# Moving weight conversion from the middle of a chunked recurrence into its last steps

## Chip, cores and metric

One core of a Trainium2 chip runs the whole kernel. The metric is the device time in microseconds; the kernel before has a median of 979.26 us over three runs (976.2 to 980.47).

## What is computed

Three layers follow one another. The first is a recurrence over 768 positions with a 40x40 state for each of 4 batches x 8 heads; the second a feed-forward layer with a three-tap convolution and a gate; the third an FFT mixing, a normalisation and a second feed-forward layer.

```python
def _attn_ref(r, k, v, w, a, b):                       # B, H, S, D = 4, 8, 768, 40
    for t in range(S):
        y[:, :, t] = np.einsum('bhd,bhde->bhe', rt, state)
        Sa = np.einsum('bhde,bhe->bhd', state, at)
        state_decay = state * wt[:, :, None, :] - np.einsum('bhd,bhe->bhde', Sa, bt)
        state = state_decay + np.einsum('bhd,bhe->bhde', vt, kt)

def _moe_ref(x, w_in, conv_w, w_out):                  # x: 4 x 768 x 320, w_in: 320 x 1024
    h = np.maximum(x @ w_in, 0.0)
    ...
    for k in range(K):
        conv_out += conv_w[k][None, None, :] * hp[:, k:k + S, :]
    gate = 1.0 / (1.0 + np.exp(-conv_out))
    return (h * gate @ w_out).astype(np.float32)
```

The weights `w_in`, `w_out`, `conv_w`, `w_ch1` and `w_ch2` arrive as 64-bit floats. They are turned into 32-bit floats on the chip, and all but `w_out` and `conv_w` are split into a high and a low part.

## The kernel before, in words

**The recurrence** is cut into 12 chunks of 64 positions. `Attn.run` (its loop is at L663) makes 52 steps n = 0 to 51; step n works on batch n % 4 of chunk n // 4, and on later stages of the three items before it. `step` (L530) writes out the order of the stages: `stage_u`, `stage_h` and `stage_y` interleaved on TensorE (PE), then `stage_s` (state update: `sm` on VectorE, L452 and L456, then `st` on GpSimd, L457 and L458), `stage_g` (`gt` on VectorE, L470), `stage_sb`, `stage_ut` and `stage_o` (`xo` on VectorE, L509, stored by L513). One `gt` and one `xo` stand in each step. The inputs of a chunk's half (`vbd` L203, `z` L183, `zt` L185, `rbd` L187, `r` L191) are loaded by the SyncE queue (SP) every second step, in line with everything else that SP issues.

Beside the steps a triangular inverse for each pair of chunks runs on VectorE (`tmp` and `A`, L333 and L336; its transposes L313, L343, L346). It is spread evenly over the steps until step 40, by when the last pair needs it. After that no step has any of it.

**The conversion** is a second stream of work that `run` takes as `side`. `Moe.prep` (L731) goes through 63 pieces; 30 of them (`NLEFT` leaves 33) lie in the recurrence: 12 of `w_in` (128x256), 16 of `w_out` (128x160) and 2 of `w_ch1` (128x256). `conv_w` (L756) follows. A piece is loaded as `raw` (L765, SP), and then takes these instructions:

```python
raw = tp.tile([128, PC, 2], I32, name="raw", tag="raw", bufs=2)[:p, :w]     # L764, load L765 on SP
nc.scalar.activation(m, hi.bitcast(F32), AF.Abs)                            # L775 ScalarE, pm<-raw
nc.scalar.activation(y, lo.bitcast(U32), AF.Copy, scale=2.0 ** -29)         # L776 ScalarE, py<-raw
nc.vector.tensor_scalar(m, m, W_LEAST, W_MOST, op0=ALU.max, op1=ALU.min)    # L778 VectorE
nc.vector.tensor_scalar(m, m, 3, 0x3fffffff, ...)                           # L780 VectorE
nc.gpsimd.tensor_tensor(m, m, y, op=ALU.add)                                # L782 GpSimd, pm<-pm,py
nc.vector.scalar_tensor_tensor(m, hi, -0x40000000, m, ...)                  # L785 VectorE, pm<-raw,pm
```

A `w_out` piece is then stored by L745. A piece that is split goes on with `wh` (L749, ScalarE, stored by L750) and `wl` (L752, VectorE, stored by L753). `raw` and `pm` have two buffers, `py`, `wh` and `wl` one. The next piece's `raw` is issued when a piece starts.

`prep` is a generator with a `yield` after each group of instructions, 8 to 9 for a piece. `step` is one too, with some 8 to 10 yields a step. At each yield of a step `run` adds `SIDE` to a counter (L681), and for each whole unit in it takes one group from `side`, so `SIDE = 0.75` means three groups for four yields. A group is tied behind the last instruction marked on ScalarE and VectorE (`issue_after`). What is left of `side` when the steps are over is taken at once. A scheduler then makes each engine's order out of this program order and those ties; all engines run their list in order.

**The second layer** begins with `moe1_start` (L821): `load_k320` (L798 to L802) brings the converted `w_in` back from DRAM in six transfers of 2.62 MB together, and L819 brings `w_out` (eight transfers, 1.31 MB). These tiles lie on the same side of the on-chip memory as the tiles of the conversion. `moe1` then loads `xf` (L836 to L838), makes `xh` and `xl` of it (ScalarE L839 to L841, GpSimd L842 to L844), and its first multiplication `hp<-xh,w_in_h` (L701) needs all six `w_in` tiles. `cw`, the convolution's weights, is needed by L876. The 33 pieces left are converted beside this layer.

Of the kernel before, what the change touches and what calls it, by code (L numbers as in the profile page):

```python
# [61 lines left out]
SM = 1  # L62
MG = 1
RI = 0.8
SIDE = 0.75
N1ST = 4
NA = 8
HL = 3
LG = 16
# [5 lines left out]
def turns(left, right):  # L75


    sides = []
    for stages in (left, right):
        ops = []  # L80
        for todo, end in stages:
            ops += [(op, None) for op in todo[:-1]] + [(todo[-1], end)]
        sides.append(ops)
    n = max(len(ops) for ops in sides)
    for k in range(n):
        for ops in sides:
            for op, end in ops[k * len(ops) // n:(k + 1) * len(ops) // n]:
                op()
                if end is not None:
                    end()  # L90
                    yield
# [7 lines left out]
class Attn:  # L99
# [494 lines left out]
    def run(self, side):  # L594
        nc, tc = self.nc, self.tc
        self.start()
        wm = self.pst("warm")
        for _ in range(WARM):
            nc.tensor.matmul(wm[:, 0:396], self.ends[:, 0:128], self.ends, start=True, stop=True)
        self.load_pre(0, 0)  # L600
        nc.sync.dma_start(self.mdiag, self.i["mdiag"])
        self.load_pre(0, 1)
        nc.sync.dma_start(self.mltq, self.i["mlt"])
        nc.sync.dma_start(self.ident, self.i["ident"])
        self.load_pre(1, 0)
        self.grp_start(0)
        self.decay(0, 0)
        for hb in range(2):
            if hb:
                self.decay(0, 1)  # L610
            for bl in range(2):
                self.gram(0, 2 * hb + bl)
        for hb in range(2):
            self.load_v(0, hb)
        self.pads()
        for hb in range(2):
            self.load_z(0, hb)
            self.load_r(0, hb)
        inv = self.inverse(0)
        for n in range(ST0):  # L620
            next(inv)
        for hb in range(2):
            for bl in range(2):
                self.gram_x(0, 2 * hb + bl)
        with tc.issue_after(self.late.ins):
            for hb in range(2):
                self.squares(0, hb)
                if hb == 0:
                    self.load_pre(1, 1)
        self.grp_start(1)  # L630

        def half(hb):
            if hb < ST2:
                self.decay(1, hb)
            else:
                with tc.issue_after(self.first.ins):
                    self.decay(1, hb)
            self.squares(1, hb)
            for bl in range(2):
                self.gram(1, 2 * hb + bl)  # L640
                self.gram_x(1, 2 * hb + bl)
        half(0)
        for b in range(B):
            for _ in turns([self.stage_h(0, b)], []):
                pass
        if ST1:
            half(1)
        next(inv)
        next(inv)
        tr = self.last  # L650
        for _ in inv:
            pass
        if not ST1:
            half(1)
        live, g = [], 1
        for hb in range(2):
            self.load_v(1, hb)
        for k in range(8 - LD, 8 - LG, 2):
            h = divmod((k + LD) // 2, 2)
            self.load_pre(*h)  # L660
            with tc.issue_after(tr.ins):
                self.decay(*h)
            self.squares(*h)  # L663
        sd, na = 0.0, 8 - LG
        for n in range(B * NCH + 4):
            while live and n == live[0]["end"]:
                for _ in live.pop(0)["inv"]:
                    pass
            while g <= NCH // 2 and na + LG >= 8 * g and len(live) < 2:
                end = 8 * g - 8 if g > 1 else 4  # L670
                live.append(dict(inv=self.inverse(g), end=end, last=0, acc=0.0,
                                 rate=RI * (35 if g == 1 else 70) / 7 / max(1, end - n - MG)))
                next(live[-1]["inv"])
                g += 1
            pre = []
            for _ in range(1 + (n < NA)):
                if na <= n:
                    pre.append(self.ahead(na))
                    na += 1
            for _ in self.step(n, itertools.chain(*pre), live):  # L680
                sd += SIDE if n >= N1ST else 0.0  # L681
                while sd > 0:
                    with ExitStack() as st:
                        for m in [self.mark, self.markd][:1 + SM]:
                            if m is not None:
                                st.enter_context(self.tc.issue_after(m.ins))
                        next(side, None)
                    sd -= 1.0
                for k, v in enumerate(live):
                    v["acc"] += v["rate"]  # L690
                    while v["acc"] > 0 and not (v["last"] == "t" and k or v["last"] in ("merge", "join", "done")):
                        v["last"] = next(v["inv"], None)
                        v["acc"] -= 1.0
        for _ in side:
            pass
# [714 lines left out]
```

## Time and profile before

| what | value |
|---|---|
| median of three runs | 979.26 us |
| profiled execution | 977.45 us, span 975.5 us |
| PE busy | 818.7 us (84% of the span) |
| VectorE (DVE) busy | 668.3 us (69%) |
| ScalarE (ACT) busy | 519.7 us (53%) |
| GpSimd (POOL) busy | 433.2 us (44%) |
| first `up` of the recurrence | 72.1 us |
| first `hp` of the second layer | 478.0 us |
| mean granted clock of PE | 0.925 of full speed |

Busy shares of the whole span mix three layers with different limits, so the table serves to find the stages; each stage is read by itself. L12 is line 12 of the kernel; a `pm<-pm` is an instruction that writes the tile `pm` from the tile `pm`. SPq is SyncE, which issues the transfers. In brackets behind a row of a timeline stands how long the engine had been idle before it and what ended that.

### The profile page before, as it was taken

The page shows a single profiled execution, that of the slowest core. Times are in us where ns is not written, and L with a number is a line of the kernel's source. Part 1 is how long each engine was busy: PE and PEld are TensorE (multiplying, and loading weights), DVE is VectorE, ACT ScalarE, POOL GpSimd, SP SyncE. Part 2 cuts the span into 40 slices and gives each one's busy share as a digit, 9 for nine tenths or more (in the row PEclk, how much of TensorE's full clock was granted, in tenths as well). Part 3 has the DMA queues.
Part 4 walks back from the last instruction along what each step waited for, and adds up shares of the span by engine and source line. Part 5 has one row for each costly group of instructions (what it writes and reads, how often), then busy time and mean ns, then how long its engine had stood idle before and what let it go on. Part 6 is the DMA issues. An engine that isn't in the chain of part 4 may idle for free. (4 is left out here: it accounts for less than half of the span.)

```text
span 975.5 us, 21804 instructions
## 1 busy us (share of the span) xinstructions
PE 818.7 (84%) x8178; PEld 745.1 (76%) x8178; DVE 668.3 (69%) x1320; ACT 519.7 (53%) x1448; POOL 433.2 (44%) x507
## 2 busy tenths in 40 slices
PE   5457765776886787877899899899999999999997
PEld 3446655676776787776877677777889999999997
DVE  6994897998997898942378688788773544424321
ACT  4747685577676785543566665656553321312211
POOL 5465355465565553532368557665662130101000
PEclk8758797898898999988999999999999999999999
DMA  9623262566564654539444643213004000000001
GB/s 231 187 57 108 80 172 72 167 172 164 162 175 109 172 138 114 159 101 262 121 123 111 208 122 92 79 29 94 14 26 151 22 1 21 21 21 22 21 14 32
DMA packets 102990, 101.16 MB, mean 104 GB/s; under 512 B 47272, under 2 KB 89115, under 8 KB 102875
## 3 DMA queue, kind: packets, MB, share of 16 engines
q1 hardware_dynamic: 100907, 94.73, 34.7%
q0 software_dynamic: 1968, 4.93, 1.7%
q8 instruction: 67, 1.10, 0.5%
q14 instruction: 48, 0.39, 0.1%
HBM read 74.81 MB, written 20.76 MB: 98 GB/s over the span
## 5 line engine op out<-in xcount | busy, mean ns | idle before, releaser
L1132 DVE SCALAR_TENSOR_TENSOR gl<-hp,gh 128x384 fp32r<-128x384 f32 x80 | 44.4, 556 | 111.3 <-ACT gh L1131 111.2
L895 PE MATMUL acc<-w_out_f,z 128*128 128x320 f32 x384 | 116.6, 441 | 3.6 <-POOL z L882 2.1
L1131 ACT ACTIVATE gh<-hp 128x384 fp32r<-128x384 f32 x80 | 39.3, 492 | 149.7 <-PE hp L701 149.6
L878 DVE SCALAR_TENSOR_TENSOR c<-h,cw,c 128x384 f32<-128x384 f32 x128 | 101.6, 798 | 17.3 <-ACT c L876 15.4
L895 PEld LDWEIGHTS acc<-w_out_f,z 128*128 128x128 f32 x384 | 72.1, 193 | 28.2 <-POOL z L882 3.9
L701 PE MATMUL hp<-xh,w_in_h 128*128 128x386 f32 x192 | 76.4, 398 | 12.1 <-ACT h L869 11.9
L701 PE MATMUL hp<-uh,w_ch_h 128*128 128x384 f32 x240 | 82.3, 343 | 0.0
L701 PE MATMUL hp<-ul,w_ch_h 128*128 128x384 f32 x240 | 81.0, 337 | 0.0
L388 PE MATMUL yp<-x,gt 128*64 128x40 f32 x768 | 64.9, 244 | 18.8 <-DVE gt L470 18.4
L1155 POOL DMA_INDIRECT out<-o,rows x12 | 11.8, 982 | 150.8 <-DVE o L1150 131.9
L388 PEld LDWEIGHTS yp<-x,gt 128*64 128x64 f32 x768 | 60.0, 148 | 21.4 <-DVE gt L470 21.4
L219 PE MATMUL gram<-abd,kb 120*128 120x192 f32 (+1 forms) x288 | 59.5, 353 | 17.8 <-DMA a<-in_a 11.2
L1145 PE MATMUL acc<-w_ch_h,gh 128*128 128x320 f32 x240 | 73.2, 312 | 0.0
L1145 PE MATMUL acc<-w_ch_l,gh 128*128 128x320 f32 x240 | 73.0, 309 | 0.0
L333 DVE TENSOR_TENSOR tmp<-A 128x30 f32<-128x30 f32 (+9 forms) x150 | 70.1, 467 | 3.1
L219 PEld LDWEIGHTS gram<-abd,kb 120*128 120x128 f32 x288 | 55.1, 224 | 19.4 <-issue 11.6
L336 DVE TENSOR_TENSOR A<-A,tmp 128x30 f32<-128x30 f32 (+9 forms) x150 | 67.3, 449 | 2.9
L701 PE MATMUL hp<-xl,w_in_h 128*128 128x386 f32 x192 | 67.4, 351 | 0.0
L388 PE MATMUL gp<-rbd,zt 120*128 120x192 f32 (+1 forms) x288 | 59.0, 347 | 7.1 <-ACT zt L437 4.0
L782 POOL TENSOR_TENSOR pm<-pm,py 128x160 int32<-128x160 int32 (+2 forms) x64 | 44.4, 693 | 41.2 <-DVE pm L780 22.3
L879 ACT ACTIVATE c<-c 128x384 f32<-128x384 f32 x64 | 33.4, 521 | 53.9 <-DVE c L878 53.5
L1145 PE MATMUL acc<-w_ch_h,gl 128*128 128x320 f32 x240 | 61.4, 309 | 0.0
(225 smaller groups left out, 2565.0 us busy)
## 6 DMA issues: line engine op xcount, KB each, us to landing
kb<-in_kb SPq DMA_DIRECT2D x24, 360.0 KB
vbd<-in_vbd SPq DMA_DIRECT2D x24, 320.0 KB
xd<-xo SPq DMA_DIRECT2D x56, 90.0 KB
w<-in_w SPq DMA_DIRECT2D x24, 185.6 KB
a<-in_a SPq DMA_DIRECT2D x24, 180.0 KB
z<-in_zv SPq DMA_DIRECT2D x24, 180.0 KB
zt<-in_vt SPq DMA_DIRECT2D x24, 180.0 KB
rbd<-in_r SPq DMA_DIRECT2D x72, 60.0 KB
```

The source lines that it names most:

```text
L219: nc.tensor.matmul(gp[:, 192 * gi:192 * gi + 64 * nh], d["kb"][:, bl * NG + gi].rearrange("p a b -> p (a b)"), abd[:, 0:nh, bl * NG + gi], ...
L333: nc.vector.tensor_tensor(tmp, A[:, s + 1:32, s:s + 1].to_broadcast([128, n, s]), A[:, s:s + 1, 0:s].to_broadcast([128, n, s]), op=ALU.mult)
L336: nc.vector.tensor_tensor(A[:, s + 1:32, 0:s], A[:, s + 1:32, 0:s], tmp, op=ALU.add)
L388: self.lastpe = op(*args, **kw)
L701: nc.tensor.matmul(out, l, r, start=(j == 0), stop=(j == len(ops) - 1))
L782: nc.gpsimd.tensor_tensor(m, m, y, op=ALU.add)
L878: nc.vector.scalar_tensor_tensor(c, h[:, j:HS + j], cw[:, f, j:j + 1], c, op0=ALU.mult, op1=ALU.add)
L879: nc.scalar.activation(c, c, AF.Sigmoid)
L895: nc.tensor.matmul(self.acc[t][:, 0:DM], z[:, ts], w[:, f], start=(f == 0), stop=(f == NF1 - 1))
L1131: self.mark = nc.scalar.activation(gh, hp[:, 0:HS], AF.Relu)
L1132: nc.vector.scalar_tensor_tensor(gl, hp[:, 0:HS], 0.0, gh.bitcast(F32), op0=ALU.max, op1=ALU.subtract)
L1145: nc.tensor.matmul(self.acc[t][:, 0:DM], l[:, ts], r, start=(f == 0 and j == 0), stop=(f == NF2 - 1 and j == 2))
```

## The change

Two constants are changed and two are new. Up to step 7 no group of the conversion is taken (before: up to step 3); from step 8 to 37 the counter rises by 0.37 a yield, from step 38 on by 2.2.

```diff
-SIDE = 0.75
-N1ST = 4
+SIDE = 0.37
+SIDE2 = 2.2
+N1ST = 8
+N2ST = 38
...
             for _ in self.step(n, itertools.chain(*pre), live):
-                sd += SIDE if n >= N1ST else 0.0
+                sd += (SIDE if n < N2ST else SIDE2) if n >= N1ST else 0.0
                 while sd > 0:
```

No instruction is added or left out; every engine has the same ones in another order. Lines of the changed kernel that lie behind the constants are two higher (L470 becomes L472).

VectorE, around the 29th `gt` of the recurrence, where an inverse ends (L343, L346; `A` and `t` are the inverse's tiles). Before:

```order
L452 TENSOR_TENSOR sm_112<-sp,mdiag 120x240
L456 TENSOR_TENSOR sm_112<-sp,mdiag 80x80
L778 TENSOR_SCALAR pm<-pm 128x160
L780 TENSOR_SCALAR pm<-pm 128x160
L470 TENSOR_TENSOR gt<-gp,mlt 128x512
L343 STREAM_TRANSPOSE t_4951<-A 128x32x32
L346 STREAM_TRANSPOSE tt_132<-A 128x32x32 x2
L509 TENSOR_TENSOR xo<-yt,wx 120x192
L785 SCALAR_TENSOR_TENSOR pm<-raw,pm 128x160
L452 TENSOR_TENSOR sm_112<-sp,mdiag 120x240
```

The same place now:

```order
L454 TENSOR_TENSOR sm_112<-sp,mdiag 120x240
L458 TENSOR_TENSOR sm_112<-sp,mdiag 80x80
L472 TENSOR_TENSOR gt<-gp,mlt 128x512
L345 STREAM_TRANSPOSE t_4777<-A 128x32x32
L348 STREAM_TRANSPOSE tt_132<-A 128x32x32 x2
L511 TENSOR_TENSOR xo<-yt,wx 120x192
L787 SCALAR_TENSOR_TENSOR pm<-raw,pm 128x256
L454 TENSOR_TENSOR sm_112<-sp,mdiag 120x240
```

Two instructions of the conversion have left the row ahead of `gt`, and the piece in hand is one of `w_in` (256 wide), where before it was one of `w_out`. Counted over the lists, 96 of the conversion's VectorE instructions stand before the 36th `gt` in the kernel before (12 pieces of `w_in` and 16 of `w_out`), and 44 in the changed one (11 of `w_in`).

VectorE, in one of the last steps, from an `xo` on. Before:

```order
L509 TENSOR_TENSOR xo<-yt,wx 120x192
L452 TENSOR_TENSOR sm_112<-sp,mdiag 120x240
L456 TENSOR_TENSOR sm_112<-sp,mdiag 80x80
L470 TENSOR_TENSOR gt<-gp,mlt 128x512
L509 TENSOR_TENSOR xo<-yt,wx 120x192
```

Now:

```order
L511 TENSOR_TENSOR xo<-yt,wx 120x192
L787 SCALAR_TENSOR_TENSOR pm<-raw,pm 128x160
L780 TENSOR_SCALAR pm<-pm 128x160
L782 TENSOR_SCALAR pm<-pm 128x160
L787 SCALAR_TENSOR_TENSOR pm<-raw,pm 128x160
L454 TENSOR_TENSOR sm_112<-sp,mdiag 120x240
L458 TENSOR_TENSOR sm_112<-sp,mdiag 80x80
L472 TENSOR_TENSOR gt<-gp,mlt 128x512
```

Four to five VectorE instructions of the conversion stand in each of these steps now, one and a half pieces, where none stood. From the 39th `gt` to the 48th and last the changed list has 46 of them.

SP, at the end of the recurrence, where the weights of the second layer are loaded (`w_in_h_6705` and the like are the on-chip tiles). Before:

```order
L513 DMA xd_62<-xo 120x3x64
L191 DMA r<-in_r 120x384
L798 DMA w_in_h_6705<-w_in_h 128x1024
L798 DMA w_in_h_6706<-w_in_h 128x1024
L799 DMA w_in_h_6707<-w_in_h 64x1024
L800 DMA w_in_h_6707<-w_in_l 64x1024
L802 DMA w_in_l_6704<-w_in_l 128x1024
L802 DMA w_in_l_6703<-w_in_l 128x1024
L819 DMA w_out_f<-w_out_h 128x320
L513 DMA xd_62<-xo 120x3x64
L819 DMA w_out_f<-w_out_h 128x320 x2
L203 DMA vbd<-in_vbd 128x640
```

Now:

```order
L767 DMA raw<-in_conv_w 128x48
L752 DMA w_ch_h<-wh 128x256
L755 DMA w_ch_l<-wl 128x256
L838 DMA xf<-xd_62 128x2x386
L839 DMA xf<-xd_62 64x386
L515 DMA xd_62<-xo 120x3x64 x3
L1174 DMA ident_6682<-in_ident 128x128
L840 DMA xf<-xd_62 64x386
L752 DMA w_ch_h<-wh 128x256
L755 DMA w_ch_l<-wl 128x256
L767 DMA raw<-in_w_ch 128x512 x2
L800 DMA w_in_h_6705<-w_in_h 128x1024
```

The loads of `w_in` stood between the recurrence's own loads and stores, ahead of the last ten `xd` stores, those of `w_out` soon behind them. Now all of them stand behind the last `xd` store, behind the last two stores of the conversion and behind the first two `raw` of the pieces that are left.

## Rows read from the trace of the kernel before

**Rows 1.** Stretches: us; busy of PE, PEld, DVE, ACT, POOL; clock; DMA share; GB/s.

```profile
105.60:404.00 298.40, 227.00 (x3516) 208.78 (x3518) 269.54 (x566) 202.63 (x642) 158.09 (x179) 0.89 0.53 143
...
430.20:453.00 22.80, 22.60 (x417) 20.89 (x412) 8.16 (x22) 13.01 (x36) 8.62 (x13) 1.00 0.78 223
453.00:466.00 13.00, 6.05 (x66) 5.25 (x64) 1.05 (x2) 3.36 (x8) 2.41 (x3) 0.66 0.85 220
```

**Rows 2.** Waits of DVE, 105.6 to 404: in total, times, longest (us).

```profile
DVE A L313 <- ACT l L236: 14.2, 5, 6.3
```

**Rows 3.** Waits of PE, 105 to 404.

```profile
PE sp L388 <- DVE xo L509: 20.6, 14, 4.3
```

**Rows 4.** The same for instructions on `pm` alone: DVE, ACT, POOL.

```profile
105.60:404.00 298.40, 48.77 (x96) 16.18 (x41) 18.83 (x28) 0.89 0.53 143
```

**Rows 5.** Single lines, 268 to 404: shortest, median, longest (ns).

```profile
L778 DVE TENSOR_SCALAR pm<-pm x15: 226/362/1054, 273.8 to 399.2; 128x160 f32<-128x160 f32 x15
...
L780 DVE TENSOR_SCALAR pm<-pm x15: 209/244/997, 275.9 to 400.4; 128x160 int32<-128x160 int32 x15
...
L785 DVE SCALAR_TENSOR_TENSOR pm<-raw,pm x16: 298/394/1050, 269.1 to 402.4; 128x160 int32<-128x160 int32 x16
```

**Rows 6.** Waits of PE, then of ACT, 453 to 478.

```profile
PE u L388 <- ACT hbd L412: 2.5, 1, 2.5
PE gp L388 <- DMA rbd<-in_r: 2.2, 1, 2.2
PE hu L388 <- DMA vbd<-in_vbd: 2.2, 1, 2.2
...
ACT xh L839 <- DMA xf<-xd: 9.5, 1, 9.5
```

**Rows 7.** One late step without conversion: busy time by engine.

```profile
443.90:448.00 4.10, 4.10 (x71) 3.78 (x65) 1.58 (x5) 2.10 (x7) 1.68 (x3) 1.00 1.02 226
```

**Rows 8.** Timeline of SP, then of ACT, at one `w_out` piece.

```profile
303.18 0.41 SPq L765 DMA_DIRECT2D raw<-in_w_out  x1
...
305.99 0.34 ACT L775 ACTIVATE pm<-raw 128x160 f32<-128x160 f32 x1 [2.43 <-DMA raw<-in_w_out]
306.24 0.33 ACT L776 ACTIVATE py<-raw 128x160 int32<-128x160 uint32 x1
```

**Rows 9.** Timeline of DVE in the late step of rows 7.

```profile
446.69 0.41 DVE L452 TENSOR_TENSOR sm<-sp,mdiag 120x240 f32<-120x240 f32 x1 [2.22 <-PE sp L388]
```

**Rows 10.** Timeline of POOL at the first `xf`.

```profile
463.90 1.82 POOL L842 TENSOR_TENSOR xl<-xf,xh 128x772 fp32r<-128x772 f32 x1 [10.59 <-ACT xh L839]
465.68 1.00 POOL L843 TENSOR_TENSOR xl<-xf,xh 64x386 fp32r<-64x386 f32 x1
466.75 1.00 POOL L844 TENSOR_TENSOR xh<-xf,xl 64x386 fp32r<-64x386 f32 x1
```

**Rows 11.** Timeline of PE where the second layer begins.

```profile
477.87 0.19 PE L574 MATMUL rp<-ro,rs 120*1 120x1 f32 x2
477.99 0.45 PE L701 MATMUL hp<-xh,w_in_h 128*128 128x386 f32 x1
```

**Rows 12.** Timeline of SP at that place.

```profile
478.09 0.44 SPq L1172 DMA_DIRECT2D ident<-in_ident  x1
...
479.07 0.92 SPq L765 DMA_DIRECT2D raw<-in_w_ch  x2
```

**Rows 13.** Timeline of SP at the `w_in` loads.

```profile
438.37 0.88 SPq L798 DMA_DIRECT2D w_in_h<-w_in_h  x2
439.34 0.50 SPq L799 DMA_DIRECT2D w_in_h<-w_in_h  x1
439.88 1.35 SPq L800 DMA_DIRECT2D w_in_h<-w_in_l  x1
441.28 1.10 SPq L802 DMA_DIRECT2D w_in_l<-w_in_l  x2
```

**Rows 14.** Transfers in 438.3 to 451.

```profile
DMA packets 2101, 3.58 MB, mean 282 GB/s; under 512 B 941, under 2 KB 1439, under 8 KB 2099
```

## The prediction

> **What bounds the kernel now.** I read the stretches first, since the change moves work only inside the recurrence and at its end. From 105.6 to 404 us VectorE is busy for 269.5 of 298.4 us, 90%, while PE has 227 and ScalarE 203 [rows 1]. Its longest wait there is 14.2 us in five pieces, for the first instruction of the five inverses [rows 2], and PE's longest waits are for VectorE: 20.6 us until an `xo` is done [rows 3]. So VectorE bounds this stretch, and an instruction taken off it shortens the stretch by about its own time. From 430.2 to 453 it is the other way: PE is busy for 22.6 of 22.8 us and VectorE for 8.2 [rows 1]. A step there takes 4.1 us, of which VectorE works 1.6, ScalarE 2.1 and GpSimd 1.7 [rows 7]. There is idle time on all three, in pieces. From 453 to 466 neither is busy: PE works 6 of 13 us [rows 1] and waits three times, 2.2 us for `vbd`, 2.2 us for `rbd`, 2.5 us for a copy on ScalarE; ScalarE itself had stood 9.5 us before the cast of `xf` [rows 6]. These are loads of the recurrence that share the queue and the transfer engines with `w_in` and `w_out`, which SP issues from 438.4 us on [rows 13]. They pay for something: the second layer's first multiplication starts 0.1 us behind the recurrence's last on PE [rows 11].
>
> **The change, part by part.** The instructions stay the same, so four things count: what leaves the VectorE-bound stretch, what stall goes, what the late steps pay, and what happens to the `w_in` loads.
>
> *A, steps 4 to 37.* Up to the 36th `gt` 52 of 96 VectorE instructions of the conversion leave. All 96 together take 48.8 us, 508 ns each [rows 4], so the upper end is 52 x 0.508 = 26.4 us. But what leaves is in kind all 16 `w_out` pieces and one of `w_in`, and a `w_out` piece's three instructions take 226 + 209 + 298 = 733 ns at their shortest, against medians of 362, 244 and 394 [rows 5]. What lies above the shortest comes from work beside them and can pass to the next VectorE instruction. So the lower end is 17 x 0.73 = 12.5 us. GpSimd's part of these pieces leaves too, 17 x 18.83/28 = 11.4 us, but that is 7% of its 158 us [rows 1, 4], so most of what stretches VectorE's instructions stays. I take 16 us, nearer to the lower end. At 90% that is **-14 us**, between -11 and -24.
>
> *S, the stall.* Without `w_in` and `w_out` in that queue the three waits of 453 to 466 (6.9 us) have no cause, nor has the half clock behind them: the granted clock is 0.66 there, so 6 us of PE work would take 4 [rows 1, 6]. **-9 us**, with 0 as the other end if the late conversion delays the same loads.
>
> *B, the late steps.* One and a half pieces now stand in each of some ten steps, 46 VectorE instructions. Where room is enough they cost nothing: VectorE's gap in a late step is 2.2 us [rows 9], and 1.5 pieces need 1.5 x 0.73 = 1.1 us of it; ScalarE's two instructions of a piece are 0.67 us [rows 8] of its 2.0 idle. That is the lower end, 0. But a piece is a chain over three engines, and only two `raw` exist. From the issue of a `raw` to its first use went 2.8 us [rows 8]. Then come ScalarE 0.67, VectorE 0.44, GpSimd 0.67, VectorE 0.30 [rows 4, 5, 8], and only then the next `raw` of that buffer: 4.9 us for two pieces, 2.4 a piece, 3.7 us for 1.5 pieces. That fits 4.1, just. With one place in line on each of the three engines, 0.4 to 0.9 us each, it is 6.9 us for two and 5.2 us a step, 11 us over ten steps. Who waits then is not the conversion alone: behind its instruction on ScalarE stand the copies of `hbd` and `sb`, on GpSimd the update of `st`, and PE waits for these; on SP the chunk's `vbd`, `z`, `rbd` and `zt` stand behind a store that waits for VectorE. Beside this, the three GpSimd instructions on the first `xf`, 3.8 us [rows 10], now stand between two updates of `st`; some 2 us of them don't fit. I take 5 + 2 = **+7 us**, between 0 and +18.
>
> *C, the second layer's start.* In the changed order of SP the six `w_in` loads stand behind the last `xd`, behind the last piece's two stores and two `raw`. In the kernel before SP issued the two `raw` at 479.07 us for 0.92 us, 1.2 us after PE's last `rp` at 477.87 [rows 11, 12]; the two stores and a piece of `xf` ahead of them add some 1.5 us with the copies that they wait for. So the first `w_in` is issued some 3.5 us after the recurrence's end. The six issues take 4.0 us [rows 13], beside the transfer. At 282 GB/s, which the transfers had while these loads ran [rows 14], 2.62 MB take 9.3 us, and from issue to first use of a small one went 2.8 us [rows 8], 0.4 of them the issue, 0.6 its own bytes; call the rest 2. Sum 3.5 + 2 + 9.3 = 15 us in which PE has nothing to do, where it had 0.1. Behind waits of 2 us its clock was granted at 0.66 [rows 1]; behind 15 us it will fall too, and I add 2 us for a first unit at half clock. **+17 us**, between +13 and +20. `w_out` follows behind and is needed three units later; `cw` is done in the gap.
>
> A rule speaks on the same price. The Trainium skill ("DMA: Bandwidth & Descriptors", section "Anatomy of one DMA") fits a transfer as 2.0 us plus its bytes at 436 GB/s; by that the 2.62 MB would be there in 8.0 us instead of 11.3, C would be 3 us smaller, and the sum -2 instead of +1. The trace moved less with its other traffic, 282 GB/s, and no row shows these loads by themselves, so the sum keeps the row.
>
> *Sum:* -14 - 9 + 7 + 17 = **+1 us**. Against the profiled execution's 977.45 us that is 978.5; the median of the three runs lies 1.8 us above it and would come to 980.3. I write **979.5**. The three runs differ by 4.3 us, so about 0.5% (4.9 us) is what can be told from no change. The forecast is that the change can't be told from none: two gains of 23 us in the recurrence are handed back, mostly at the seam to the second layer.
>
> **The rivals.**
>
> *Slower: the late conversion sets the pace.* Mechanism B at its upper end. It decides once 1.5 pieces need more than a step's 4.1 us, that is over 2.7 us a piece with two `raw`; the unhindered chain is at 2.4. For it: no late step has any idle time on PE [rows 7], so each wait counts in full, and in the VectorE-bound stretch ScalarE once stood 2.4 us for a `raw` [rows 8]. Against it: the gaps on all three engines are there. B = +16 and S only -6 give -14 - 6 + 16 + 17 = +13: **991.5 us**.
>
> *Faster: A in full.* If the stretched VectorE instructions are stretched because of GpSimd instructions that hold them up, and both leave together, then A is its lower end and GpSimd's time on top, 12.5 + 11.4 = 24 us, close to 52 times the mean: -24 instead of -14. For it: the spread in rows 5, where the longest `pm<-pm` is 1054 ns against 226 at the shortest. Against it: 93% of GpSimd's work stays. With the rest unchanged the sum is -9: **970 us**. The Trainium skill states this mechanism ("SBUF — State Buffer", section "Who interferes with whom"): VectorE and GpSimd share a pair of ports as an exclusive lock, and whoever comes second is blocked for the other's whole instruction. By that rule this rival would be the likelier; the rows show the stretching, but not whose instruction it was.
>
> *The change does not do what it says.* The rates act on the program's order, and a scheduler could have put the groups elsewhere. The lists exclude this: 52 instructions do leave the first 36 `gt`, and 46 do stand in the last ten steps. What could fail is the late rate: 2.2 groups a yield, if the chain can't follow, only lengthens the tail, which is the slower rival.
>
> **How the numbers follow.** The forecast, within 0.5% of before, has 0.36; the slower rival 0.33, since both its causes (tight chain, idle PE at the seam) are in the lists; the faster one 0.31. The range reaches from the faster case with a shorter seam (970 - 4) to the slower one with a longer seam (991.5 + 2.5): **966 to 994**. The forecast's own range is 974.5 to 984.5. Faster by over 0.5%: 0.31; within: 0.36; slower: 0.33.
>
> **What would show it.** In the changed profile the 36th `gt` should stand 11 to 24 us earlier, with VectorE still busy for about 90% of the stretch and its conversion instructions down to 44 in it. The three waits for `vbd`, `rbd` and `hbd` should be gone. The late steps should lie between 4.1 and 5.2 us, with PE waits under 1 us in each. Between `rp` and the first `hp` there should be 13 to 18 us in which PE waits for `w_in`, and half clock behind it. I am wrong if the first `hp` follows at once, if the stretch up to 404 us shortens by under 8 us, or if single steps after the 38th take over 6 us.

## The result and the profile after

The changed kernel takes **987.9 us** (median of 6 runs, 984.1 to 988.9); the kernel before, on the same chip, 979.9 (6 runs, 976.2 to 984.1). The ratio is **1.0087, 95% interval 1.0064 to 1.0111**: slower by 0.9%. The number lies inside the range of the prediction, but the forecast, no change that can be told, is not what came. The time is that of the slower rival.

Of the two profiled executions the one of before has a span of 975.5 us, the one of after 986.7, so 11.2 us are to be found. Four marks in the trace cut them up: the 36th `gt` (end of the VectorE-bound stretch), PE's last `rp` (end of the recurrence), the fifth unit of the second layer (its fifth group of `hp`), and the last `hp` of that layer.

| from, to | before | after | difference | term, as predicted |
|---|---|---|---|---|
| start, 36th `gt` | 404.3 | 390.8 | -13.5 | A: -14 |
| 36th `gt`, `rp` | 73.6 | 78.9 | +5.3 | S and B: -9 + 7 |
| `rp`, fifth unit | 7.9 | 24.1 | +16.2 | C: +17 |
| fifth unit, last `hp` of the layer | 229.9 | 232.7 | +2.8 | 0 |
| last `hp`, end | 259.8 | 260.2 | +0.4 | 0 |

Steps are counted here by their `gt`: step 41 runs from the 40th `gt` to the 41st. First the stretches of the changed kernel, as in rows 1: the VectorE-bound one, then steps 39 and 40, steps 41 to 44, the last four with `rp`, and the seam to the second layer (us; busy time and instructions of PE, PEld, DVE, ACT, POOL; granted clock; DMA share; GB/s).

```profile
105.60:390.50 284.90, 230.69 (x3512) 213.08 (x3514) 246.39 (x507) 193.39 (x608) 149.63 (x162) 0.87 0.50 135
400.90:422.90 22.00, 18.09 (x406) 16.59 (x402) 14.87 (x31) 12.17 (x32) 9.18 (x13) 0.77 0.40 109
422.90:447.40 24.50, 19.73 (x260) 17.94 (x260) 14.52 (x37) 14.09 (x42) 15.25 (x23) 0.86 0.73 205
447.40:469.70 22.30, 18.47 (x207) 16.48 (x207) 9.86 (x32) 10.36 (x33) 4.51 (x8) 0.85 0.55 144
471.30:491.80 20.50, 7.21 (x21) 6.60 (x22) 3.25 (x5) 2.68 (x6) 2.95 (x6) 0.50 0.88 267
```

Against [rows 1] VectorE has 23.2 us less to do in the first stretch (269.5 to 246.4), and the stretch is only 13.5 us shorter: VectorE's idle time in it went from 28.9 to 38.5 us. In the late steps it is the other way: steps 41 to 44 took 16.4 us before (from the 40th `gt` at 435.2 to the 44th at 451.6) and take 24.5, with PE busy for 19.7. Single steps take 10.9 and 11.1 us (39 and 40; 6.4 and 9.1 before) and then 7.7, 6.4, 4.3 and 6.1. At the seam PE works 7.2 of 20.5 us, at a granted clock of 0.50, which is 1.2 GHz.

VectorE's longest waits in the first stretch, as in rows 2:

```profile
DVE xo L511 <- PE yt L390: 13.3, 6, 6.0
DVE A L315 <- ACT l L238: 4.6, 4, 2.2
DVE t L345 <- POOL A L342: 4.3, 3, 2.1
```

The wait for the first instruction of the inverses fell from 14.2 us [rows 2] to 4.6, but a new one of 13.3 us stands ahead of `xo`, for PE. The conversion's instructions alone (line by stretch; busy time of DVE, ACT and POOL, then clock, DMA share and GB/s):

```profile
105.60:390.50 284.90, 22.23 (x44) 9.81 (x23) 8.26 (x11) 0.87 0.50 135
400.90:469.70 68.80, 21.38 (x56) 6.47 (x19) 10.02 (x19) 0.83 0.57 154
422.90:447.40 24.50, 9.24 (x20) 2.44 (x7) 3.67 (x7) 0.86 0.73 205
```

In the first stretch 44 are left of 96, 22.2 us of 48.8 [rows 4]. In steps 41 to 44 there are 20, or 6.7 pieces of three: 3.7 us a piece. From 400.9 to 469.7 us the longest waits of ScalarE, VectorE, GpSimd and PE:

```profile
ACT pm L777 <- DMA raw<-in_w_out: 16.8, 9, 3.4
...
DVE pm L780 <- ACT pm L777: 13.1, 8, 3.4
DVE pm L787 <- POOL pm L784: 8.6, 13, 1.0
...
POOL pm L784 <- DVE pm L782: 12.9, 5, 5.4
POOL pm L784 <- ACT z L429: 10.1, 5, 4.4
...
PE yp L390 <- DVE gt L472: 4.7, 3, 3.3
PE bp L390 <- DVE t L345: 3.7, 1, 3.7
```

ScalarE, VectorE and GpSimd each stand longest at an instruction of the conversion, and PE stands for VectorE. One such place in the order of time, on SP, ScalarE, VectorE and PE (start, duration, engine, line, instruction, idle time before it and what ended it):

```profile
426.65 0.57 SPq L767 DMA_DIRECT2D raw<-in_w_out  x1
...
429.75 0.34 ACT L777 ACTIVATE pm<-raw 128x160 f32<-128x160 f32 x1 [3.10 <-DMA raw<-in_w_out]
...
430.12 0.24 DVE L780 TENSOR_SCALAR pm<-pm 128x160 f32<-128x160 f32 x1 [2.61 <-ACT pm L777]
430.40 0.24 DVE L782 TENSOR_SCALAR pm<-pm 128x160 int32<-128x160 int32 x1
430.56 0.68 DVE L472 TENSOR_TENSOR gt<-gp,mlt 128x512 f32<-128x512 f32 x1
...
431.30 0.33 PE L390 MATMUL yp<-x,gt 128*64 128x40 f32 x1 [3.33 <-DVE gt L472]
```

A load of 164 KB is issued at 426.65 and used 3.1 us later. ScalarE stands for it, VectorE stands for ScalarE, and `gt`, which is in line behind two conversion instructions on VectorE, is late; PE stands for 3.3 us. `gt` itself needed none of the conversion's data.

The seam, on SP and PE:

```profile
473.95 0.88 SPq L767 DMA_DIRECT2D raw<-in_w_ch  x2
474.88 0.90 SPq L800 DMA_DIRECT2D w_in_h<-w_in_h  x2
...
477.19 1.18 SPq L804 DMA_DIRECT2D w_in_l<-w_in_l  x2
...
469.66 0.19 PE L576 MATMUL rp<-ro,rs 120*1 120x1 f32 x2
480.13 0.66 PE L703 MATMUL hp<-xh,w_in_h 128*128 128x386 f32 x1 [10.28 <-DMA w_in_h<-w_in_h]
...
486.22 0.69 PE L703 MATMUL hp<-xh,w_in_l 128*128 128x386 f32 x1 [4.47 <-DMA w_in_l<-w_in_l]
```

The first `w_in` load is issued 5.2 us behind `rp`, the last of the six tiles is in use 11.3 us later. PE stands for 10.3 and then 4.5 us, where it stood 0.1 us before [rows 11].

### The profile page after: what moved, and what is told of

Same layout as the page of the kernel before. It is cut to its first block, busy times and chain, and to the rows that moved or that the text cites. A ratio compares the mean times of both kernels' runs of the same rounds, so it can differ in the third digit from the quotient of the medians.

```text
span 986.7 us, 21819 instructions
## 1 busy us (share of the span) xinstructions
PE 831.6 (84%) x8178; PEld 757.6 (77%) x8178; DVE 664.3 (67%) x1320; ACT 520.8 (53%) x1448; POOL 432.4 (44%) x507
## 5 line engine op out<-in xcount | busy, mean ns | idle before, releaser
L390 PE MATMUL yp<-x,gt 128*64 128x40 f32 x768 | 67.5, 249 | 19.6 <-DVE gt L472 18.1
L390 PEld LDWEIGHTS yp<-x,gt 128*64 128x64 f32 x768 | 62.7, 153 | 22.7 <-DVE gt L472 22.6
L390 PE MATMUL gp<-rbd,zt 120*128 120x192 f32 (+1 forms) x288 | 61.3, 356 | 5.0 <-ACT zt L439 4.9
L459 POOL TENSOR_TENSOR st<-st,sm 120x360 f32<-120x360 f32 x40 | 43.0, 1074 | 43.5 <-DVE sm L458 27.3
L703 PEld LDWEIGHTS hp<-xh,w_in_h 128*128 128x128 f32 x192 | 38.1, 199 | 31.1 <-ACT h L871 17.1
```

Of the source, the lines that this page charges most:

```text
L390: self.lastpe = op(*args, **kw)
L459: nc.gpsimd.tensor_tensor(self.st[b], self.st[b], t, op=ALU.add)
L703: nc.tensor.matmul(out, l, r, start=(j == 0), stop=(j == len(ops) - 1))
```

## The experiments

Four points were to be told apart: what the late conversion costs and by which step of its chain; whether the seam is `w_in` lying over the conversion's tiles; what the stall of 453 to 466 us in the kernel before came from; and whether the rates can gain anything once these are mended. The 36th `gt` stood at 390.8 to 393.4 us in the six profiles with the change's conversion up to there (the change and runs 1 to 5), 392.3 in the mean, and at 402.4 to 405.7 in the four with that of the kernel before, 404.0 in the mean. So a mark in one profile is good to some 3 us, and stretches are compared between marks of one profile. Where a kernel is compared in time, it is with the kernel before on the same chip.

**1. No conversion in the late steps.**

```diff
-SIDE2 = 2.2
+SIDE2 = 0.0
...
-        for _ in side:
-            pass
+        with self.tc.issue_after(self.mark.ins), self.tc.issue_after(self.markd.ins):
+            for _ in side:
+                pass
```

> The changed kernel, but the part of the conversion that is left at the 38th step is held back until the recurrence's last step is done. Theory (the late conversion slows the late steps): from the 36th to the 48th gt should come down from 75.3 us to about 62 (70.8 of the kernel before less its 8.6 us stall), steps 41 to 44 from 24.5 us to 16.4, and the last rp should stand at about 456 us instead of 469.7. The 15 pieces then stand in the open behind it at 2 to 2.8 us each, so the time is 1005 to 1017 us. Rival (something else slows the late steps: the casts of the first xf, the clock, the other order of the loads): the 36th to the 48th gt stay at 73 to 76 us, and the time is above 1017.

Measured: 1017.2 us, ratio 1.0359 (1.0323 to 1.0394). The two `gt` and the seam:

```profile
392.75 0.68 DVE L472 TENSOR_TENSOR gt<-gp,mlt 128x512 f32<-128x512 f32 x1
...
454.19 0.69 DVE L472 TENSOR_TENSOR gt<-gp,mlt 128x512 f32<-128x512 f32 x1 [2.04 <-PE gp L390]
...
456.96 0.19 PE L576 MATMUL rp<-ro,rs 120*1 120x1 f32 x2
512.58 0.66 PE L704 MATMUL hp<-xh,w_in_h 128*128 128x386 f32 x1 [55.43 <-DMA w_in_h<-w_in_h]
```

The time is 0.2 us past the theory's upper end; the marks are the theory's and not the rival's. From the 36th to the 48th `gt` it is 61.4 us (62 expected), to `rp` 64.2 against 78.9 in the change. So **the late conversion costs 14.7 us**. The casts of `xf` and the place of the `w_in` loads are as in the change, and the clock follows the waits: 0.92 between the two `gt`, where it was 0.85. Steps 41 to 44 come to 19.8 us, not 16.4, since step 43 takes 7.5 us, 3.4 more than 4.1. In it GpSimd's three instructions on the first `xf` stand ahead of the state update:

```profile
429.73 1.82 POOL L845 TENSOR_TENSOR xl<-xf,xh 128x772 fp32r<-128x772 f32 x1 [2.95 <-DMA rbd<-in_r]
...
433.67 0.94 POOL L459 TENSOR_TENSOR st<-st,sm 120x360 f32<-120x360 f32 x1
```

Against the 73.6 us of the kernel before, the 64.2 us are 9.3 less. That is a sum: steps 45 and 46, where the stall was, fell from 17.2 to 7.0 us (10.2 less), steps 37 to 40 together took 2.5 us less, and the step with `xf` took 3.4 more.

Behind `rp` this run shows the conversion with nothing beside it. ScalarE's first instruction of every second `w_out` piece:

```profile
475.12 0.34 ACT L778 ACTIVATE pm<-raw 128x160 f32<-128x160 f32 x1 [2.87 <-DMA raw<-in_w_out]
...
479.99 0.34 ACT L778 ACTIVATE pm<-raw 128x160 f32<-128x160 f32 x1 [2.94 <-DMA raw<-in_w_out]
...
484.99 0.34 ACT L778 ACTIVATE pm<-raw 128x160 f32<-128x160 f32 x1 [3.06 <-DMA raw<-in_w_out]
```

Two pieces take 4.9 us there, or 2.5 a piece, store included, where they take 3.7 a piece among the steps. So the chain with its two `raw` is 2.5 of the 3.7, and the rest is what the steps add to it.

**2. and 3. A third `raw`.** `wh` and `wl` hold nothing while `w_out` is converted; a third `raw` lies over them, and loads are issued two pieces ahead. In the first of the two runs `wh` and `wl` are one tile in the second layer too, in the second run only in the recurrence.

```diff
-            if len(self.pieces) > left:
-                raw = self.load_raw(tp, self.pieces[0][0], *self.pieces[0][2:])
+            while len(raws) < min(1 + (left > 0 and len(d) == 1), len(self.pieces) - left):
+                s = self.pieces[len(raws)]
+                nw += len(s[1]) == 1
+                raws.append(self.load_raw(tp, s[0], *s[2:], left and len(s[1]) == 1 and nw % 3 == 0))
...
+        if third:
+            raw = tp.tile([128, PC, 2], I32, name="raw3", tag="whl", bufs=1)[:p, :w]
```

> The changed kernel with a third raw buffer for the w_out pieces (it lies over wh and wl, which those pieces do not use) and loads issued two pieces ahead instead of one. Theory (a piece's chain from the issue of its raw on, with two raw, sets the pace of the late steps): ScalarE's waits for raw between 400.9 and 469.7 us fall from 18.7 to under 5 us, steps 41 to 44 from 24.5 to 19 to 21 us, and the time by 4 to 6 us to 982 to 984. Rival (it is the places in line on ScalarE, VectorE and GpSimd, not the load): the waits for raw go but the idle time comes back as waits for pm and py, steps 41 to 44 stay above 23 us, and the time stays at 986.5 to 989.5.

Measured: 988.8 us, 1.0099 (1.0061 to 1.0136), the rival's number, and steps 41 to 44 at 23.1 us are the rival's too; of its waits those for the stores of `w_out_h` came, 8.4 us. But the recurrence did gain: from the 36th `gt` to `rp` it is 73.5 us, and the time from the first `hp` with `w_ch` to the end rose from 257.0 to 263.0 us. That is where the joined tile is still in use; without it there:

> The run with the third raw buffer once more, with wh and wl joined in one tile in the recurrence alone, so that the conversion of the second layer's time is that of the changed kernel. In the run before, the recurrence's end (rp) came 3.5 us earlier, but from the first hp with w_ch to the end it took 263.0 us against 257.0. Theory (the loss of 6 us behind the recurrence came from the joined tile, the load of raw costs the late steps some 5 us of their 14): from the 36th gt to rp 73 to 75 us against 78.9, from the first hp with w_ch to the end 257, the time 981.5 to 984.5 us. Rival (the late steps gain, but the seam takes it back): 986.5 to 989.

Measured: **980.5 us, 1.002 (1.000 to 1.004)**, 7.4 us less than the change. From the 36th `gt` to `rp` it is 72.3 us, with 22.1 for steps 41 to 44, and the time behind the first `hp` with `w_ch` is 257.8, so the loss was the joined tile's. ScalarE's longest waits from the 36th `gt` to `rp`:

```profile
ACT pm L786 <- DMA w_out_h<-pm: 5.9, 6, 1.9
ACT hbd L413 <- PE hu L390: 4.4, 3, 2.4
ACT pm L786 <- issue: 2.7, 1, 2.7
ACT py L787 <- POOL pm L793: 2.5, 4, 0.9
ACT py L787 <- DMA raw<-in_w_out: 2.1, 1, 2.1
```

The waits for a `raw` of `w_out` fall from 16.8 to 2.1 us, and **6.6 of the 14.7 us go with them**. The next link shows at once: with `raw` there, ScalarE stands for the store of `w_out_h`, which holds one of the two `pm`. The remaining 8 us are this and the places in line together; they were not taken apart.

**4. `w_in` off the conversion's tiles.**

```diff
-                with tc.tile_pool(name="b_w", bufs=1, reuse_waits="tile", side="right") as wp, \
+                with tc.tile_pool(name="b_wo", bufs=1, reuse_waits="tile", side="right") as wop, \
+                        tc.tile_pool(name="b_w", bufs=1, reuse_waits="tile", side="right") as wp, \
...
-        self.wo = [wp.tile([128, NF1, DM], F32, name="w_out_f")]
+        self.wo = [wop.tile([128, NF1, DM], F32, name="w_out_f")]
```

> The changed kernel with w_out_f in a pool of its own over the tiles of the conversion, and w_in in a pool beside it that lies over the tiles of the inverses only. The w_in loads then are issued from about the 39th step on. Theory (at the seam the second layer waits for w_in, whose tiles lie over those of the conversion): the first hp follows rp by 1 to 3 us instead of 10.4, from rp to the fifth unit it takes 9 to 13 us instead of 24.1 (w_out is then awaited there), and the time falls by 11 to 15 us to 973 to 977. Rival 1 (the loads now collide with raw and the chunks' loads): the late steps take 5 to 9 us more, the time is 979 to 986. Rival 2 (the seam is not the w_in loads but xf or cw): unchanged, 987 to 989.

Measured: **973.4 us, 0.9927 (0.9899 to 0.9956)**, faster than both kernels. SP and PE:

```profile
421.89 0.86 SPq L800 DMA_DIRECT2D w_in_h<-w_in_h  x2
...
470.64 0.19 PE L576 MATMUL rp<-ro,rs 120*1 120x1 f32 x2
470.76 0.45 PE L703 MATMUL hp<-xh,w_in_h 128*128 128x386 f32 x1
```

`w_in` is issued in step 40 and `hp` follows `rp` at once; the fifth unit comes 8.9 us behind `rp` instead of 24.1. The late steps pay nothing for the loads in sum: 77.2 us from the 36th `gt` to `rp`, against 78.9. So the seam was the place of the tiles, and it cost 15 us.

**5. Both edits together.**

> Both edits, the pools and the third raw. If the late chain and the seam are two separate costs, the gains add: 967 to 973 us. If the loads of w_in take from the raw loads what the third buffer gives, it is the time of the run with the pools alone, within 2 us.

Measured: 985.0 us, 1.0043 (1.0026 to 1.0059): worse than the pools alone, which neither expectation had. The joined tile is in this run too (264.8 us behind the first `hp` with `w_ch`, against 257.2 with the pools alone), and the late stretch is longer besides, 82.2 us in the profiled execution, which was the slowest of the six at 990.3: beside the `w_in` loads ScalarE stands 12.4 us for the stores of `w_out_h`, once 6.1, where it stood 8.4 in run 2. It may be that the deeper prefetch and `w_in` stand ahead of the stores that free `pm`; that was not tried by itself.

**6. to 8. Other rates over the two pools, and the pools without the change.**

> The two pools (w_in over the inverses' tiles), with rates 0.55 from step 4 and 1.1 from step 38 in place of 0.37 from step 8 and 2.2: 72 conversion instructions of VectorE up to the 36th gt (96 before, 44 in the change), about 3 a step behind it instead of 4.6. Theory (the late price grows with the pieces a step, and a piece a step nearly fits): the 36th gt at 396 to 399 us, from there to rp 69 to 73 us (77.2 with the pools and the change's rates), the time 966 to 972. Rival (the late price is paid by the w_in loads beside the steps, whatever the number of pieces): from the 36th gt to rp stays at 76 to 78, the time is 975 to 980.

Measured: 979.5 us, 0.9988 (0.9965 to 1.0011), a miss: the 36th `gt` stands at 400.2, from there to `rp` it is 74.6 us, with a step of 11.1 us behind the 42nd `gt`, and the fifth unit comes 12.5 us behind `rp`, 3.6 later than with the pools and the change's rates.

> The two pools with one rate of 0.62 from step 4 to the end: 81 conversion instructions up to the 36th gt, about 2 a step behind it. Theory: the 36th gt at 398 to 401 us, from there to rp 66 to 71 us, the time 966 to 973. Rival as for the run with 0.55 and 1.1: 976 to 981.

Measured: 973.2 us, 0.9935 (0.9901 to 0.9968); from the 36th `gt` (402.7) to `rp` 69.6 us, with a step of 12.4.

> The kernel before with the two pools alone. Its w_in loads are issued behind the conversion's end beside steps 43 to 46 in either case, so if the pools help the changed kernel only because its conversion lasts to the end, nothing changes here: 977 to 983 us. If the pools were a gain of their own, as with the change's rates, it would be 965 to 970.

Measured: 976.7 us, 0.9966 (0.9947 to 0.9984): a gain of 0.3%, so the pools gain what they do in run 4 because the change's conversion lasts to the end. Step 44 takes 13.6 us here. In the long step of all three ScalarE waits for `xf`, 4.5, 7.2 and 8.4 us. The run with 0.62, ScalarE first, then PE:

```profile
444.55 0.83 ACT L841 CAST xh<-xf 128x772 fp32r<-128x772 f32 x1 [7.16 <-DMA xf<-xd]
445.29 0.28 ACT L413 COPY hbd<-hu 64x160 f32<-64x160 f32 x1
445.59 0.28 ACT L414 COPY hbd<-hu 64x160 f32<-64x160 f32 x1
...
445.92 0.40 PE L390 MATMUL u<-hbd,tt 128*64 128x80 f32 x1 [5.61 <-ACT hbd L414]
```

ScalarE stands at the first cast of `xf` for its load, the copies of `hbd` stand behind it, and PE behind these.

**9. to 12. The casts of the first `xf` held back.** They are put behind a mark of a late step (46 in the edit shown, which is over the change; 47 in the two runs over the kernel before):

```diff
+            if (b, hf) == (0, 0) and self.hold is not None:
+                hs.enter_context(self.tc.issue_after(self.hold.ins))
...
+            moe.hold = att.marks[46]
```

> The kernel before with one edit: ScalarE's three casts of the first xf are held back until a late mark of step 47 of 52, some two steps later. In the kernel before, ScalarE stands 9.5 us at the first of these casts for xf, and the copies of hbd stand behind it. Theory 1 (the stall of 453 to 466 us comes from the w_in and w_out loads that make vbd, rbd and xf late, as the prediction had it): steps 45 and 46 stay at 15 to 17 us together, the time stays within 2 us of before. Theory 2 (the stall is mostly that cast standing ahead of hbd in ScalarE's order, whatever makes xf late): steps 45 and 46 fall to 7 to 10 us together and the time falls by 4 to 8 us, to 972 to 976.

Measured: 976.8 us, 0.9971 (0.9955 to 0.9987). Steps 45 and 46 take 13.0 us against 17.2, between the theories. PE's waits from 452.6 to 465.6 us in this run, and the stretch itself:

```profile
PE gp L388 <- DMA rbd<-in_r: 1.9, 1, 1.9
PE hu L388 <- DMA vbd<-in_vbd: 0.9, 1, 0.9
...
452.60:465.60 13.00, 10.15 (x121) 9.11 (x118) 2.04 (x5) 4.31 (x12) 1.54 (x2) 0.74 0.82 203
```

So some 4 us of that stall are the cast's place in ScalarE's order, and the rest is late loads, 2.8 us of waits in these rows, as the prediction had it, with a clock of 0.74 on top. The time falls by 2.0 us only: the first `hp` comes 2.8 us earlier, the last `hp` of the layer 0.2.

> The run with the two pools and the one rate of 0.62, and the casts of the first xf held back to step 46. In that run one step of 12.4 us remains (8.3 us over the others), and ScalarE stood 7.2 us for xf there with hbd behind it. Theory 2: that stall goes, the time is 963 to 967 us. Theory 1 (the loads themselves are late): it moves to vbd or rbd, the time stays at 971 to 974.

Measured: **968.5 us, 0.9899 (0.9876 to 0.9922)**. The time lies between the theories. The long step is gone, steps 45 and 46 take 9.1 us instead of 7.0, and from the 36th `gt` to `rp` it is 66.8 us.

> The kernel before with the two pools and the held casts. With the pools alone a step of 13.6 us remained, 9.5 us over the others, with ScalarE standing 8.4 us for xf. Theory 2: 966 to 969 us. Theory 1: 975 to 978.

Measured: 976.3 us, 0.9975 (0.9962 to 0.9988): here theory 1 holds. Step 44 fell from 13.6 to 4.1 us, but steps 45 and 46 rose from 7.0 to 13.5: PE waits there 2.4 us for `vbd` and 1.3 for `rbd`, so most of the stall only moved.

> The run with the pools, the rate of 0.62 and the held casts, with the third raw buffer as well. With 2 VectorE instructions a step the chain of a piece has room, so if the raw load costs late steps only where pieces are dense, nothing is gained: within 2 us of the run without it. If the raw load costs at this rate too, it is 3 to 5 us faster.

Measured: **967.4 us, 0.9883 (0.9864 to 0.9903)**, within 2 us of the run without the third `raw`, as expected for sparse pieces. These two runs with 0.62 and the held casts are the fastest, 1.0 to 1.2% under the kernel before, and not told apart.

## Why the prediction was right and wrong

**A (-14, came as -13.5): right in sum, by luck; its two parts are each off.** The price of an instruction that leaves was taken near its shortest. It was the other end: 52 conversion instructions took 26.5 us less, the mean of 510 ns, and VectorE's whole busy time fell by 23.2, so its other instructions took 3.3 us more. But only 58% of that shortened the stretch, or half by the means of all profiles, whose 36th `gt` are 11.7 us apart. The 90% for the share on the path was the weak step: with VectorE relieved, other waits came up (`xo` for PE, 13.3 us where it was 2.7), VectorE's idle time rose by 9.6 us and its busy share fell from 90 to 86%.

That the mean would leave with the instructions was the faster rival's first half, and it is borne out; its time was not, since the path moved. Its reason, that GpSimd holds the stretched instructions up, is borne out too, as far as traces can show it without a run that takes GpSimd's part away alone. In three stretches (that of rows 4, and the first two of the changed kernel's conversion rows above) 72 of the conversion's VectorE instructions take longer than any of the same form beside which GpSimd does nothing. Each of the 72 ends 0.1 to 0.3 us behind a GpSimd instruction, and 71 of them began while that one was running. One of them, on VectorE, and the GpSimd instruction beside it, in the kernel before:

```profile
355.26 1.05 DVE L778 TENSOR_SCALAR pm<-pm 128x160 f32<-128x160 f32 x1
...
354.96 1.26 POOL L338 TENSOR_SCALAR_AFFINE_SELECT A<-A 128x1024 f32<-128x1024 f32 x1 [1.65 <-DVE A L336]
```

The first ends at 356.3, 0.1 us behind the second; without GpSimd beside it such an instruction takes 0.23 us. The trace agrees so far with the rule of the Trainium skill that stood with that rival ("SBUF — State Buffer", section "Who interferes with whom"), by which whoever comes second is blocked for the other's whole instruction. It does not in eight more cases, where a GpSimd instruction began up to 0.4 us earlier by the profile and VectorE's was not stretched.

**S (-9): right.** All three waits are gone, and the two steps that held them take 10.2 us less in run 1. That run 1's whole stretch is 9.3 us shorter than before is the sum of that with two things that S did not hold, the 2.5 and 3.4 us named there. That it was the `w_in` and `w_out` loads alone was too simple: run 9 shows 4.2 of 17.2 us as ScalarE's cast standing ahead of `hbd`.

**B (+7; the conversion's 5 came as 14.7): this term failed.** The unhindered chain, "4.9 us for two pieces, 2.4 a piece", was right: run 1 shows 4.9 behind `rp`. The step that failed was to take a value near that chain, because it "fits 4.1, just". With one place in line on each engine the prediction had 6.9 us for two and 11 us over ten steps, and took 5 of them. Measured are 3.7 us a piece, 7.4 for two, so the limit of 2.7 us that the slower rival named was passed. And more than the slower pieces is paid: the engines take their instructions in order, so the wait for a load on ScalarE goes through VectorE's line into `gt`, which is not part of the chain: the wait of 3.1 us for `raw` became 3.3 us on PE. The prediction named this risk for the copies of `hbd` and `sb` and the update of `st`, and priced it as slower pieces instead of as waits of PE. These were forecast under 1 us a step; they are up to 3.3, and 3.7 at an inverse's transpose. The prediction's own sign of being wrong came, steps of over 6 us. That its chain left out the store that frees `pm` cost nothing as long as `raw` is what ScalarE waits for; with `raw` mended (run 3) this store is next. The 2 us for the first `xf` came as 3.4 in run 1; with them B is 18, the upper end of its bounds of 0 to +18 (18 less the 10.2 and 2.5 us of run 1 is the table's +5.3).

**C (+17, came as +16.2): right**, by nearly its own working: from the first issue to the last use 11.3 us, where 2 us and 9.3 us at 282 GB/s were reckoned, and 5.2 us instead of 3.5 from `rp` to that issue. PE's waits are 10.3 and 4.5 us, 14.8 together where 15 were reckoned, in two parts and not one. The fit of the Trainium skill ("DMA: Bandwidth & Descriptors", section "Anatomy of one DMA") gave 8.0 us; the page gives it for one transfer issued by way of GpSimd, while these are six, issued by SP, and the trace differs, with 267 GB/s over the seam. Run 4 shows the cause.

**Not in the sum: +2.8 us in the second layer.** Around 555 us ScalarE stands 2.2 us at a `wh` for the store that held it (0.3 us at the same place before), the copy of `h` is behind it, and PE's clock is granted at 0.50 for 6.8 us, where it was so for 3.4 before. The `w_ch` conversion fell otherwise against the units; this was read and not tried.

The table's sum is -13.5 + 5.3 + 16.2 + 2.8 + 0.4 = 11.2 us. With the stretch of S and B at its measured +5.3 the prediction's sum would have been +8, or 988: the slower rival's case, to which it had given 0.33.

## What to carry to other kernels

Background work in an in-order line is not priced by its busy time: follow one piece from the issue of its load to the store that frees its last buffer and divide by the buffers. That is what a piece takes alone (2.5 us here); among the steps a place in line on every engine comes on top (3.7), and above what a step has room for, each wait is paid by whatever stands behind it on the same engine, though it needs nothing of the piece. Before work is moved to the end of a phase, look at what the next phase puts over its tiles: in the changed kernel a second pool was worth 15 us.

## What the runs showed that was not expected

The same kind of instruction had two prices. The 52 conversion instructions that left the VectorE-bound stretch, 48 of them of `w_out`, had taken 510 ns each; the 56 of the late steps, mostly the same ones, take 382. The traces tell why: in the VectorE-bound stretch of the kernel before GpSimd was at work beside 60 of the 96 conversion instructions, which took 649 ns in the mean, and the other 36 took 286; in the late steps of the changed kernel it was beside 20 of 56, at 616, and the other 36 took 271. The price with and without GpSimd is about the same in both places, and the share beside GpSimd differs.

With the pools and the held casts, one rate of 0.62 beats 0.75 from step 4 on by 8 us (968.5 to 976.3; the casts are held to step 46 in the one and 47 in the other), though 0.75 ends the conversion around the 41st `gt` and 0.62 spreads it to the end of the recurrence. The change's own rates were not tried with the held casts.
